# Where the maxima of the first softmax are taken: VectorE alone, or ScalarE, GpSimd and VectorE in turn

## The chip, the cores and the metric

The kernel runs on one core of a Trainium2 chip. The core has five engines that run beside each other: TensorE (PE in the profile) for matrix products, VectorE (DVE), ScalarE (ACT), GpSimd (POOL), and SyncE (SP), which here only issues DMAs. Each works through its own queue in order. PE writes to PSUM; GpSimd reads and writes SBUF only. The metric is the device time of one execution in microseconds; lower is better.

## The reference

Two parts. First, for each of 4 batches of 12,416 tokens with 128 channels, an attention by way of 32 inducing points:

```python
def mab(q, kv):
    s = scale * (q @ kv.transpose(0, 2, 1))
    s = s - s.max(-1, keepdims=True)
    a = np.exp(s)
    a /= a.sum(-1, keepdims=True) + 1e-09
    return a @ kv
h = mab(I, x)          # 32 points read all tokens: the first softmax
y = mab(x, h)          # all tokens read the 32 results: the second softmax
```

Second, on all 49,664 rows of y, a gated layer of width 1536:

```python
gate = 1.0 / (1.0 + np.exp(-(y @ w_gate)))
out = (gate * (y @ w_val)) @ w_out
```

## The kernel before

Tokens come in chunks of 128, 97 to a batch: six groups of 16 chunks and one chunk left over. The first softmax of a batch ("stage 1") runs over whole groups: the scores of 16 chunks stand in one PSUM bank as 128 rows (four times 32 points) by 512 columns. `s1_max` (line 264) has VectorE take the negated maximum of each row, `s1_exp` has ScalarE take the exponential with that maximum as bias, a DMA on SP's queue transposes the result (`s1_turn_dma`, line 304), PE sums it against the tokens (`s1_sum_pe`, line 315), and ScalarE copies the sum to `hst` (line 330). Each group keeps its own maximum; `plan_combine` (line 416) later joins the seven with weights, for which VectorE takes `ml` and GpSimd does the small steps up to `hx` and `e32l`. PE (line 455) and VectorE (`li`, line 375) finish it.

The second softmax ("stage 2", `plan_stage2`, line 617) takes 16 chunks too. PE scores a group in two halves (line 483); in the slot called `take` ScalarE copies the scores to `sc` (line 520) and GpSimd subtracts the greatest of each 32 by a tree of subtract, clamp and add (`s2_lower_pool`, lines 530 to 535); in the slot `weigh` ScalarE takes the exponential (line 544); one slot on, GpSimd sums (line 552); three slots on, it inverts and spreads the result to four copies `a2n` (lines 576 to 598); five to eight slots on, SP issues the transposing DMA to `a2r` (line 609).

The gated layer is the main loop. It has 97 blocks of four chunks, each block 12 columns of 128 hidden units, cut into steps of two columns and one column in turn. A step t is: PE fills the value bank `v` of step t and the gate bank `g` of step t+2 (line 944), VectorE forms u = (t16 + 1) * v (line 981), ScalarE takes the tanh of gate t+2 into `t16` (line 962), and PE multiplies earlier products u by `w_out` (line 1062). At the end of a block ScalarE copies the sum to `o` (line 1081) and SP sends it out (line 1083). Two steps are one slot, four slots a block, 96 slots a batch.

The order of all queues is written out by hand. `at(slot, make, late)` puts work into a slot: the early kind is issued after the slot's first step, the late kind after its second. Within a slot the order is that in which the work was planned, and an engine's queue keeps it. Stage 1 of batch b+1 is planned into the loop of batch b, as are the loads of `xn` on GpSimd's queue (line 96), the transposes of `xn` to `xT` on SP's queue (line 105), stage 2 of groups 0 and 1 of batch b+1, and the joining. Stage 1 of the first batch is a prologue with an order of its own, and the loop's last batch has no stage 1; so the loop has 18 full groups of stage 1. In the last batch nine columns go `aside`: ScalarE and GpSimd form them in place of VectorE (lines 1015 to 1031).

Slots below are counted from the start of a batch's loop. What the steps of the prediction need of the old plan, for the first two batches: joining starts in slot 52 and `li` stands in slot 63; the loads of slot 60 are two; group 0 of the next batch is lowered in slot 70 and weighed in slot 78.

Of the kernel before, what the change touches and what calls it, by code (L numbers as in the profile page):

```python
# [9 lines left out]
F32 = mybir.dt.float32  # L10
F16 = mybir.dt.float16
BF16 = mybir.dt.bfloat16
AF = mybir.ActivationFunctionType
ALU = mybir.AluOpType
AX = mybir.AxisListType

AFTER = mybir.DependencyInfo(mybir.DependencyClass.Sync, mybir.DependencyReason.DATA)
P = 128
GC = 16
BC = 4  # L20
ASIDE = {3: ((2, 9, 3, 8), (11, 17, 7, 1), (23, 26, 7, 0), (50, 53, 15, 3), (58, 62, 19, 11), (64, 69, 19, 10), (73, 76, 20, 5), (78, 81, 23, 11), (83, 88, 23, 10))}
LATE = (4, 19, 32, 46, 43)
NEG = 1.0e30
PROLOGUE = """
    xt 0 0, xt 0 8, cp 0 8 act, cp 0 0, w 2 1, xt 1 0, cp 1 0, sc 0, mx 0, ex 0, sc 6, xt 1 8,
# [12 lines left out]
def kernel(  # L38
# [9 lines left out]
    nc = tc.nc  # L48
# [18 lines left out]
    bp = ctx.enter_context(tc.tile_pool(name="bp", bufs=2))  # L67
    s1p = ctx.enter_context(tc.tile_pool(name="s1p", bufs=4))
    s2p = ctx.enter_context(tc.tile_pool(name="s2p", bufs=2))
    up = ctx.enter_context(tc.tile_pool(name="up", bufs=6))  # L70
    tp = ctx.enter_context(tc.tile_pool(name="tp", bufs=4))
    op = ctx.enter_context(tc.tile_pool(name="op", bufs=4))

# [158 lines left out]
    def at(slot, make, late=False, side=False):  # L232
        plan.setdefault((slot, "side" if side else late), []).append(make)
# [98 lines left out]
    def plan_stage1(b, s, score, total):  # L332
        st = {}
        full = groups[s][1] == GC

        def begin():
# [11 lines left out]
        at(score, begin)  # L348
        at(score + 1, weigh, late=full)
        at(score + 2, turn)  # L350
# [266 lines left out]
    def plan_stage2(b, c, score, take, weigh, far=None, soon=False):  # L617
        st = {}
        n = GC + (NLO if far is not None else 0)

        def bank():
            st["s2"] = ps.tile([P, GC, m], F32, tag="m", name="s2_ps")

        def room():
            st["sc"] = s2p.tile([P, GC + NLO, m], F32, tag="sc", name="sc", bufs=1)

        def one():
            room()
            bank()
            s2_score(b, 0, 0, NLO, st["s2"], True)  # L630

        def half(j0, whole):
            if j0 == 0:
                bank()
            s2_score(b, c, j0, j0 + GC // 2, st["s2"], whole)
            if soon and j0:
                st["hl"] = s2_max(GC, st["s2"])

        def lower():
            if far is None:  # L640
                room()
            s2_take(st["sc"], 0, GC, st["s2"])
            s2_lower_pool(n, st["sc"])

        def exp():
            st["e"] = s2_exp(GC, st["s2"], *st["hl"]) if soon else s2_exp_low(n, st["sc"])

        def total():
            st["sme"] = s2_sum_pool(n, st["e"])

        def spread():
            rs = (s2_inverse if soon else s2_inverse_pool)(n, st["sme"])
# [437 lines left out]
    for b in range(B):  # L1090
        o = base[b]
        more = b + 1 < B

        if b == 0:
            plan_stage2(0, groups[1][0], o, None, o + 3, soon=True)
            plan_stage2(0, groups[2][0], o + 5, o + 7, o + 18)
        for s in range(3 if b == 0 else 2, NG - 1):
            k = o + (16 * s - 28 if more else LATE[s - 2])
            plan_stage2(b, groups[s][0], k, k + 2, k + (14 if more else 10))
        k = o + (56 if more else LATE[-2])  # L1100
        plan_stage2(b, groups[NG - 1][0], k, k + 2, k + 10, far=o + (52 if more else LATE[-1]))
        if not more:
            continue
        early = (
            [(9, (18, 19, 19)), (13, (27, 27, 27))]
            if b == 0
            else [(8, (15, 16, 17)), (12, (18, 19, 19))]
        )
        later = (
            [(24, (35, 35, 35)), (28, (43, 43, 43)), (40, (48, 49, 49)), (44, (50, 51, 51))]  # L1110
            if b == 0
            else [(24, (31, 31, 31)), (28, (35, 35, 35)), (40, (47, 48, 49)), (44, (50, 51, 51))]
        )
        alone = 47 if b == 0 else 43
        for s, (score, total) in enumerate(early + later + [(32, (alone, alone, alone))]):
            plan_stage1(b + 1, s, o + score, [o + e for e in total])
        plan_combine(b + 1, o + 52, o + 55, [(o + 72, o + 74), (o + 80, o + 82)])
        plan_stage2(b + 1, groups[0][0], o + 67, o + 70, o + 78)
        plan_stage2(b + 1, groups[1][0], o + 84, o + 86, o + 94)
        for g in range(NS):  # L1120
            when = 3 * g if b else (3, 7, 16, 21, 31, 37, 12)[g]
            at(o + when, lambda b=b, g=g: x_transpose_dma(b + 1, g))
            if b == 0 and 0 < g < NG:
                at(o + (None, 4, 5, 17, 24, 31)[g], lambda g=g: x_load(1, g))
        if b + 2 < B:
            for g in range(NG):
                when = ((24, 33, 42, 60, 60, 82) if b else (33, 37, 60, 60, 78, 82))[g]
                at(o + when, lambda b=b, g=g: x_load(b + 2, g))
# [62 lines left out]
```

## Time and profile before

| | us |
|---|---|
| median of 3 runs | 719.72 |
| lowest, highest | 719.56, 719.85 |
| span of the profiled execution | 718.4 |
| busy PE, VectorE, ScalarE, GpSimd | 650.5, 702.4, 675.1, 445.8 |

The page gives no time for the profiled execution beside its span, from the first to the last instruction; 1.3 us lie between it and the median of the runs. In rows of the order of time, the first number is the start and the second the length, in us from the start of the span; rows of one operation that follow each other are merged (x4 is four of them), and a bracket gives the engine's idle time before the row and what ended it. In rows by group, the two numbers behind the count are the busy time in us and the mean length in ns.

### The profile page before, as it was taken

The numbers are of one execution on the slowest core, as the hardware profiler recorded it, in microseconds if no ns is written. First come the engines' busy times: TensorE is split into PE (matmuls) and PEld (weight loads), VectorE is DVE, ScalarE is ACT, GpSimd is POOL, SyncE is SP. The second block draws the span as 40 slices with busy tenths as digits, with TensorE's granted clock in tenths as the row PEclk, the third lists the DMA queues.
The fourth block names the chain that finished last, engine by engine and source line by source line (L and its number), as shares of the span: only waits on it lengthen the run. The fifth ranks groups of instructions, "written<-read, shape, count | busy, mean of one in ns | idle before, by whom it ended". The sixth has DMA issues, their size and how long they took to land.

```text
span 718.4 us, 21566 instructions
## 1 busy us (share of the span) xinstructions
PE 650.5 (91%) x8446; PEld 394.2 (55%) x8446; DVE 702.4 (98%) x872; ACT 675.1 (94%) x1019; POOL 445.8 (62%) x718
## 2 busy tenths in 40 slices
PE   8889889999998998999989988999899999999897
PEld 4455555555555555555555555555555555555555
DVE  5899999999999999999999999999999999999997
ACT  4699999999999999999999999999999999999996
POOL 4574763888653747588666266387766787676220
PEclk9999999999999999999999999999999999999999
DMA  9796696244568344335268431220222122223011
GB/s 209 115 182 130 125 165 105 75 90 106 89 133 162 80 103 92 59 79 119 66 117 161 102 75 51 70 74 31 77 60 73 46 62 67 39 75 71 35 46 46
DMA packets 118182, 65.77 MB, mean 92 GB/s; under 512 B 101408, under 2 KB 102208, under 8 KB 118080
## 3 DMA queue, kind: packets, MB, share of 16 engines
q1 hardware_dynamic: 112176, 50.90, 31.6%
q0 software_dynamic: 5584, 13.34, 10.9%
q8 instruction: 66, 1.08, 0.6%
q14 instruction: 36, 0.29, 0.1%
q10 hardware_dynamic: 320, 0.15, 0.1%
HBM read 27.80 MB, written 25.43 MB: 74 GB/s over the span
## 4 chain that ended last, share of the span: by engine, by line
PE 51%; ACT 24%; DVE 16%; issue 5%; DMA 2%; DVEq 1%; POOL 1%; ACTq 0%
PE acc_ps L1062 24%; ACT t L962 22%; PE v_ps L944 21%; DVE u L981 14%; PE g_ps L944 2%; DMA xn<-in_x_dram 2%; PE s_ps L483 2%; PE hp_ps L315 1%; ACT o L1081 1%; DVE nm L267 1%; DVEq L981 1%; ACT a1T L280 0%; PE s_ps L255 0%; POOL xn L96 0%; ACTq L962 0%
## 5 line engine op out<-in xcount | busy, mean ns | idle before, releaser
L981 DVE SCALAR_TENSOR_TENSOR u<-t,v_ps 128x1024 f16<-128x1024 f16 (+1 forms) x771 | 670.9, 945 | 1.7 <-PE g_ps L944 0.8
L962 ACT ACTIVATE t<-g_ps 128x1024 f16<-128x1024 f32 (+1 forms) x770 | 589.5, 822 | 22.2 <-ACT t L962 10.3
L944 PE MATMUL v_ps<-a2r,hwt 32*128 32x512 f16 (+1 forms) x1179 | 290.8, 371 | 56.9 <-DVE u L981 53.2
L1062 PE MATMUL acc_ps<-wo,u 128*128 128x128 f16 x4620 | 324.5, 220 | 0.9
L1062 PEld LDWEIGHTS <-u 128*128 128x128 f16 x4620 | 259.9, 98 | 89.5 <-issue 88.1
L944 PE MATMUL g_ps<-a2r,hwt 32*128 32x512 f16 (+1 forms) x1179 | 294.0, 376 | 0.0
L944 PEld LDWEIGHTS <-hwt 32*128 32x128 f16 x2382 | 93.5, 91 | 188.6 <-issue 142.2
L552 POOL TENSOR_TENSOR sum<-e 128x256 f32<-128x256 f16 (+1 forms) x23 | 15.5, 672 | 133.8 <-ACT e L544 130.0
L598 POOL TENSOR_TENSOR a2n<-e,rs 128x2048 f16<-128x2048 f16 (+3 forms) x25 | 86.8, 3474 | 4.8 <-DVE rs L570 3.1
L576 POOL TENSOR_TENSOR near<-sme,minus 128x16 f32<-128x16 f32 (+1 forms) x22 | 65.3, 2966 | 1.8
L1081 ACT ACTIVATE o<-acc_ps 128x512 f32<-128x512 f32 x96 | 58.4, 609 | 0.0
L531 POOL TENSOR_SCALAR rise<-rise 128x256 f32<-128x256 f32 (+6 forms) x110 | 51.2, 466 | 9.7
L532 POOL TENSOR_TENSOR top<-top,rise 128x128 f32<-128x128 f32 (+3 forms) x88 | 28.4, 323 | 7.3
L552 POOL TENSOR_TENSOR sum<-sum 128x128 f32<-128x128 f32 (+3 forms) x92 | 28.4, 309 | 7.2
L530 POOL TENSOR_TENSOR rise<-top 128x128 f32<-128x128 f32 (+3 forms) x88 | 27.3, 310 | 6.9
L530 POOL TENSOR_TENSOR rise<-sc 128x256 f32<-128x256 f32 (+1 forms) x22 | 16.3, 739 | 20.9 <-ACT sc L520 20.6
L1031 POOL TENSOR_TENSOR xn_spare<-xn_spare 128x512 f16<-128x512 f32 x9 | 11.4, 1270 | 22.2 <-ACT xn_spare L1029 22.0
L535 POOL TENSOR_TENSOR sc<-sc,top 128x512 f32<-128x512 f32 (+1 forms) x22 | 23.9, 1086 | 1.7
L1026 POOL TENSOR_SCALAR xn_spare<-xn_spare 128x512 f32<-128x512 f16 x9 | 13.4, 1493 | 11.2 <-ACT xn_spare L1025 11.2
L483 PEld LDWEIGHTS <-xT 128*128 128x128 f16 x388 | 13.1, 96 | 11.7 <-issue 11.3
L280 ACT ACTIVATE a1T<-s_ps,nm 128x512 f16<-128x512 f32 (+1 forms) x26 | 16.4, 630 | 3.1 <-DVE nm L267 3.0
L483 PE MATMUL s_ps<-hT,xT 128*128 128x32 f16 x388 | 18.1, 178 | 0.1
(150 smaller groups left out, 291.4 us busy)
## 6 DMA issues: line engine op xcount, KB each, us to landing
out_dram<-o SPq DMA_DIRECT2D x96, 256.0 KB, 2.2
xn<-in_x_dram POOLq DMA_DIRECT2D x18, 512.0 KB, 7.7
xn<-in_x_dram POOLq DMA_DIRECT2D x3, 544.0 KB, 6.9
xn<-in_x_dram POOLq DMA_DIRECT2D x3, 256.0 KB, 12.8
xn<-in_x_dram SPq DMA_DIRECT2D x1, 576.0 KB, 4.8
xn<-in_x_dram SPq DMA_DIRECT2D x1, 512.0 KB, 3.9
a2r<-a2n SPq DMA_TRANSPOSE x29, 4.5
wg<-in_moe_w_gate_dram POOLq DMA_DIRECT2D x1, 384.0 KB, 12.7
```

The source lines that it names most:

```text
L483: nc.tensor.matmul(s2[:, j, :], xT[b][:, c + j, :], hT16[b][:], start=(j == 0), stop=whole and j == j1 - 1, skip_group_check=True,)
L530: nc.gpsimd.tensor_tensor(out=r, in0=far, in1=near, op=ALU.subtract)
L531: nc.gpsimd.tensor_scalar_max(out=r, in0=r, scalar1=0.0)
L532: nc.gpsimd.tensor_tensor(out=top[:, 0:n, 0:w], in0=near, in1=r, op=ALU.add)
L552: nc.gpsimd.tensor_tensor(out=d[:, 0:n, :], in0=src[:, :, 0:w], in1=src[:, :, w : 2 * w], op=ALU.add)
L576: nc.gpsimd.tensor_tensor(out=near[:, 0:n], in0=sme[:, 0:n], in1=minus1[:, 0:n], op=ALU.pow)
L598: eng.tensor_tensor(out=a2n[:, 0:n, :, :], in0=e.unsqueeze(2).to_broadcast((P, n, 4, m)), in1=rs.unsqueeze(2).unsqueeze(3).to_broadcast((P ...
L944: st[what + "end"] = nc.tensor.matmul(pt[:, k, col : col + nb * P], hw[b][r : r + 32, j // 2, :], a2r[r : r + 32, o : o + nb, :].rearrange ...
L962: st["tanh"] = nc.scalar.activation(out=st["t"][:], in_=st["g"][:], func=AF.Tanh, scale=0.5)
L981: u = nc.vector.scalar_tensor_tensor(out=st["u"][:, :, c:e], in0=st["t"][:, :, c:e], scalar=1.0, in1=st["v"][:, :, c:e], op0=ALU.add, op1= ...
L1062: nc.tensor.matmul(acc[0][(i // 2) % len(acc[0])][:, i, :], u[:, ts(i, P)], wo16[:, j, :], start=(i in fresh), stop=not any(e[2] == ib and ...
L1081: nc.scalar.mul(out=o32[:], in_=acc[0][0][:], mul=0.5)
```

## The change

For 13 of the 18 groups the scores stay in PSUM only for one copy: ScalarE writes them, negated, to SBUF (`neg`, 128x512 in fp32) in the slot of the scores. GpSimd folds the 512 columns to 256, 128 and 64 by taking the smaller of two each time (`lower_tree`: subtract, clamp at zero, subtract; nine instructions). VectorE then takes the minimum of the 64 columns left (`finish`), which is the negated maximum that it took before from 512 columns. The exponential reads `neg` with scale -1 (`weigh_low`). Such a group has a list of six slots: score, minimum, exponential, and three for the sum. The other five groups keep the old way and four slots.

All slots move into one table, `TIMES`. Stage 2, the joining and the loads keep their slots. The first group of the third and of the fourth batch is scored 35 slots before the loop of the batch ahead of it begins, and so late in the batch before that; its `xT` transpose goes 38 slots before, behind whatever stands in that slot. The pools `up`, `tp` and `op` lose two, one and one buffers a tag; `neg` and `low1` have four.

```diff
+TIMES = (
+    {
...
+        "sum": ((10, 17, 26, 31, 31, 31), (14, 20, 30, 35, 35, 35), (27, 36, 42, 48, 48, 48), (28, 43, 43, 43), (40, 49, 49, 49), (44, 50, 50, 50), (32, 47, 47, 47)),
...
+        "turn": (3, 7, 16, 21, 31, 37, 12),
+    },
+    {
...
+        "sum": ((-35, -28, -6, -1, -1, -1), (2, 8, 11, 16, 16, 16), (10, 17, 26, 30, 30, 30), (14, 20, 30, 35, 35, 35), (27, 36, 42, 47, 47, 47), (44, 50, 50, 50), (32, 43, 43, 43)),
+        "join": (52, 55, (72, 74), (80, 82)),
+        "next": ((67, 70, 78), (84, 86, 94)),
+        "turn": (-38, -4, 3, 6, 14, 18, 16),
+    },
...
-    up = ctx.enter_context(tc.tile_pool(name="up", bufs=6))
-    tp = ctx.enter_context(tc.tile_pool(name="tp", bufs=4))
-    op = ctx.enter_context(tc.tile_pool(name="op", bufs=4))
+    up = ctx.enter_context(tc.tile_pool(name="up", bufs=4))
+    tp = ctx.enter_context(tc.tile_pool(name="tp", bufs=3))
+    sp = ctx.enter_context(tc.tile_pool(name="sp", bufs=1))
+    op = ctx.enter_context(tc.tile_pool(name="op", bufs=3))
...
+    def lower_tree(low, neg):
+        w, src = 2 * P, neg
+        rise1 = s2p.tile([P, (GC + NLO) * (m // 2)], F32, tag="sum16", name="rise1")
+        top1 = s2p.tile([P, (GC + NLO) * (m // 2)], F32, tag="sum16", name="top1")
+        while w >= LOW:
+            near, far = src[:, 0:w], src[:, w : 2 * w]
+            r = rise1[:, 0:w]
+            nc.gpsimd.tensor_tensor(out=r, in0=near, in1=far, op=ALU.subtract)
+            nc.gpsimd.tensor_scalar_max(out=r, in0=r, scalar1=0.0)
+            dst = low if w == LOW else top1
+            nc.gpsimd.tensor_tensor(out=dst[:, 0:w], in0=near, in1=r, op=ALU.subtract)
+            src = dst
+            w //= 2
...
+        def fill():
+            st["s1"] = s1_score_pe(b, s, "m")
+
+        def leave():
+            st["neg"] = sp.tile([P, 4 * P], F32, tag="neg", name="neg", bufs=4)
+            st["low"] = sp.tile([P, LOW], F32, tag="low1", name="low1", bufs=4)
+            nc.scalar.mul(out=st["neg"][:], in_=st["s1"][:], mul=-1.0)
+            lower_tree(st["low"], st["neg"])
+
+        def finish():
+            nm, _, col = s1_col(b, s)
+            nc.vector.tensor_reduce(
+                out=nm[:, col], in_=st["low"][:], axis=AX.X, op=ALU.min
+            )
+
+        def weigh_low():
+            nm, _, col = s1_col(b, s)
+            st["a1T"] = s1p.tile([P, 512], F16, tag="a1T", name="a1T")
+            nc.scalar.activation(
+                out=st["a1T"][:], in_=st["neg"][:], func=AF.Exp, bias=nm[:, col], scale=-1.0
+            )
+
+        if pooled:
+            done, weight, *total = total
+            at(score, fill)
+            at(score, leave, late=True)
+            at(done, finish)
+            at(weight, weigh_low, late=True)
+            at(weight + 1, turn)
+        else:
...
-            when = 3 * g if b else (3, 7, 16, 21, 31, 37, 12)[g]
-            at(o + when, lambda b=b, g=g: x_transpose_dma(b + 1, g))
+            at(o + times["turn"][g], lambda b=b, g=g: x_transpose_dma(b + 1, g))
```

More of the change, by code (lines that the diff above doesn't have):

```diff
@@ L21 @@
 ASIDE = {3: ((2, 9, 3, 8), (11, 17, 7, 1), (23, 26, 7, 0), (50, 53, 15, 3), (58, 62, 19, 11), (64, 69, 19, 10), (73, 76, 20, 5), (78, 81, 23, 11), (83, 88, 23, 10))}
-LATE = (4, 19, 32, 46, 43)
+TIMES = (
+    {
+        "late": {2: (5, 7, 18, None), 3: (20, 22, 34, None), 4: (36, 38, 50, None), 5: (56, 58, 66, 52)},
+        "sum": ((10, 17, 26, 31, 31, 31), (14, 20, 30, 35, 35, 35), (27, 36, 42, 48, 48, 48), (28, 43, 43, 43), (40, 49, 49, 49), (44, 50, 50, 50), (32, 47, 47, 47)),
[4 more added lines that the diff above has]
+    {
+        "late": {2: (4, 6, 18, None), 3: (20, 22, 34, None), 4: (36, 38, 50, None), 5: (56, 58, 66, 52)},
+        "sum": ((-35, -28, -6, -1, -1, -1), (2, 8, 11, 16, 16, 16), (10, 17, 26, 30, 30, 30), (14, 20, 30, 35, 35, 35), (27, 36, 42, 47, 47, 47), (44, 50, 50, 50), (32, 43, 43, 43)),
+        "join": (52, 55, (72, 74), (80, 82)),
+        "next": ((67, 70, 78), (84, 86, 94)),
+        "turn": (-38, -4, 3, 6, 14, 18, 16),
+    },
+    {
+        "late": {2: (4, 6, 14, None), 3: (19, 21, 29, None), 4: (32, 34, 42, None), 5: (46, 48, 56, 43)},
+    },
+)
+LOW = 64
 NEG = 1.0e30
@@ L330, in s1_sum_keep, with plan_stage1 @@
         nc.scalar.copy(out=hsts[b % 2][0:R, at_col[s], 0:width], in_=hp[0:R, 0:width])
[L332 removed]
+    def lower_tree(low, neg):
[11 more added lines that the diff above has]
+            w //= 2
+    def plan_stage1(b, s, score, *total):
         st = {}
         full = groups[s][1] == GC
+        pooled = len(total) > 3
         def begin():
@@ L346, in turn @@
                 st["a1"] = s1_turn_copy(s, s1_turn_pe(b, s, st["a1T"]))
-        at(score, begin)
-        at(score + 1, weigh, late=full)
-        at(score + 2, turn)
+        def fill():
[15 more added lines that the diff above has]
+                out=st["a1T"][:], in_=st["neg"][:], func=AF.Exp, bias=nm[:, col], scale=-1.0
+            )
+        if pooled:
[6 more added lines that the diff above has]
+        else:
+            at(score, begin)
+            at(score + 1, weigh, late=full)
+            at(score + 2, turn)
         first, second, keep = total
@@ L1092 @@
         more = b + 1 < B
+        times = TIMES[min(b, 1) if more else 2]
         if b == 0:
             plan_stage2(0, groups[1][0], o, None, o + 3, soon=True)
[L1096 to L1101, printed above, removed]
+        for s, (*slots, far) in times["late"].items():
+            plan_stage2(b, groups[s][0], *(o + k for k in slots), far=None if far is None else o + far)
         if not more:
             continue
[L1104 to L1119, printed above, removed]
+        for s, slots in enumerate(times["sum"]):
+            plan_stage1(b + 1, s, *(o + k for k in slots))
+        plan_combine(b + 1, *(o + k for k in times["join"][:2]), [(o + f, o + k) for f, k in times["join"][2:]])
+        for s in range(2):
+            plan_stage2(b + 1, groups[s][0], *(o + k for k in times["next"][s]))
         for g in range(NS):
-            when = 3 * g if b else (3, 7, 16, 21, 31, 37, 12)[g]
-            at(o + when, lambda b=b, g=g: x_transpose_dma(b + 1, g))
+            at(o + times["turn"][g], lambda b=b, g=g: x_transpose_dma(b + 1, g))
             if b == 0 and 0 < g < NG:
```

## The prediction

> **What bounds the kernel now.** I read the page first: busy time by engine, then the chain that ended last.
>
> ```profile
> span 718.4 us, 21566 instructions
> ...
> PE 650.5 (91%) x8446; PEld 394.2 (55%) x8446; DVE 702.4 (98%) x872; ACT 675.1 (94%) x1019; POOL 445.8 (62%) x718
> ...
> PE 51%; ACT 24%; DVE 16%; issue 5%; DMA 2%; DVEq 1%; POOL 1%; ACTq 0%
> ```
>
> The chain names PE most, because every product starts from a matmul that was itself released by the product before. The busy times say who sets the pace. By stretches of the steady loop:
>
> ```profile
> 140.00:310.00 170.00, 154.45 (x2057) 93.96 (x2056) 170.00 (x204) 164.08 (x246) 110.73 (x184) 1.00 0.49 102
> ```
>
> Columns: stretch, length, then busy time and instructions of PE, weight load, DVE, ACT, POOL, then granted clock and DMA. VectorE has no idle time, ScalarE seems nearly full, GpSimd is two thirds busy, the clock is full. So VectorE work taken out of these stretches shortens them, as long as nobody arrives later than before. What one maximum costs shows in the order of time:
>
> ```profile
> 360.34 0.60 ACT L1081 ACTIVATE o<-acc_ps 128x512 f32<-128x512 f32 x1
> 367.25 0.60 ACT L1081 ACTIVATE o<-acc_ps 128x512 f32<-128x512 f32 x1
> ...
> 388.00 0.60 ACT L1081 ACTIVATE o<-acc_ps 128x512 f32<-128x512 f32 x1
> 395.52 0.60 ACT L1081 ACTIVATE o<-acc_ps 128x512 f32<-128x512 f32 x1
> ```
> ```profile
> 387.68 0.68 DVE L267 TENSOR_REDUCE nm<-s_ps 128x1 f32<-128x512 f32 x1
> 388.28 6.99 DVE L981 SCALAR_TENSOR_TENSOR u<-t,v_ps 128x512 f16<-128x512 f16 x8
> ```
>
> One output copy ends each block of four slots. A block without a maximum takes 6.91 us (1.73 a slot), one with a maximum 7.52: 0.61 more, and the next product starts 0.60 after the maximum did, though its record is 0.68 long (the ends of VectorE records overlap by 0.08).
>
> **The change, part by part.**
>
> *VectorE.* 13 maxima go, 13 minima over 64 columns in SBUF come. The two nearest reductions:
>
> ```profile
> L424 DVE TENSOR_REDUCE ml<-nm 128x1 f32<-128x7 f32 x3 | 0.5, 153 | 0.0
> L267 DVE TENSOR_REDUCE nm<-s_ps 32x1 f32<-32x128 f32 x4 | 1.1, 271 | 0.0
> ```
>
> 7 columns take 153 ns and 128 take 271, so 64 take some 0.21 us by a straight line, 0.13 without the overlap. Saved: 0.60 - 0.13 = 0.47 each, 13 x 0.47 = 6.1 us (5.3 to 6.8 with 0.19 or 0.08 for the new one).
>
> *ScalarE.* 13 copies come. How much room there is shows where ScalarE is fullest, in the last batch:
>
> ```profile
> 558.46 0.60 ACT L1081 ACTIVATE o<-acc_ps 128x512 f32<-128x512 f32 x1
> 558.94 1.53 ACT L962 ACTIVATE t<-g_ps 128x1024 f16<-128x1024 f32 x2
> 560.32 0.63 ACT L1029 COPY xn_spare<-side_v_ps 128x512 f32<-128x512 f32 x1
> ...
> 627.25 0.60 ACT L1081 ACTIVATE o<-acc_ps 128x512 f32<-128x512 f32 x1
> ...
> 634.45 0.64 ACT L1081 ACTIVATE o<-acc_ps 128x512 f32<-128x512 f32 x1
> ```
>
> A 512-column operation holds ScalarE 0.48 (558.46 to 558.94), a slot's two gates 1.38 (558.94 to 560.32). Against 1.73 a slot it has 0.35 to spare, 1.4 a block: room for the output copy and nearly two more. The 94% of the page overstates it, for the same overlap. But two extras in one block, as between 627.25 and 634.45, made 7.20 of 6.91: crowding costs up to 0.29. The 13 copies (6.2 us of ScalarE) fall mostly in blocks with none or one extra; copy, exponential and `hst` copies meet in a block about twice a batch. I take 0.6 us, ends 0 and 13 x 0.29 = 3.8. The exponential now reads SBUF instead of PSUM. The rows have 635 ns for one from SBUF and 683 from PSUM (another bias), so I count no change, ends -0.6 and +0.6 us in all, inside the ends above.
>
> ```profile
> L280 ACT ACTIVATE a1T<-s_ps,nm 128x512 f16<-128x512 f32 x22 | 15.0, 683 | 3.1 <-DVE nm L267 3.0
> L544 ACT ACTIVATE e<-sc 128x512 f16<-128x512 f32 x18 | 11.4, 635 | 0.0
> ```
>
> [...]
>
> *GpSimd.* Each tree is nine instructions on 256, 128 and 64 columns, the same three widths with which the second softmax's tree begins. One whole such stretch, and its place in GpSimd's queue around slots 60 to 79 of the first batch:
>
> ```profile
> 150.47 1.21 POOL L96 DMA_DIRECT2D xn<-in_x_dram  x2
> 152.41 0.69 POOL L552 TENSOR_TENSOR sum<-e 128x272 f32<-128x272 f16 x1 [0.74 <-ACT e L544]
> ...
> 163.03 0.73 POOL L530 TENSOR_TENSOR rise<-sc 128x256 f32<-128x256 f32 x1
> ...
> 168.54 0.24 POOL L530 TENSOR_TENSOR rise<-top 128x32 f32<-128x32 f32 x1
> ...
> 170.57 1.07 POOL L535 TENSOR_TENSOR sc<-sc,top 128x512 f32<-128x512 f32 x1
> ...
> 173.19 0.66 POOL L552 TENSOR_TENSOR sum<-e 128x256 f32<-128x256 f16 x1 [0.94 <-ACT e L544]
> ```
>
> 163.03 to 168.54: 5.5 us a tree (5.2 if flat operands run like the 128x258 addition, 644 ns instead of 733), 72 us in all. It is free wherever GpSimd waits, and mid-batch it does. At the end of a batch it does not: between 150.47 and 173.19 its only pauses are the two in brackets. The tree of the next batch's group 0 (score at -35, that is slot 61) is queued right behind the two loads of slot 60. It starts at 151.68 at best and ends at 157.2, so the sum behind it starts 4.8 late (5.5 less the 0.74 pause), and so does the lowering of `sc`, which then ends at 171.64 + 4.8 = 176.4 instead of 171.64. ScalarE's exponential of slot 78 needs it:
>
> ```profile
> 172.47 0.63 ACT L544 ACTIVATE e<-sc 128x512 f16<-128x512 f32 x1
> 172.99 1.51 ACT L962 ACTIVATE t<-g_ps 128x1024 f16<-128x1024 f32 x2
> ```
> ```profile
> 174.47 1.81 DVE L981 SCALAR_TENSOR_TENSOR u<-t,v_ps 128x1024 f16<-128x1024 f16 x2
> ```
>
> It would start at 176.4, 3.9 late. Behind it in ScalarE's queue is the gate that ends about 174.02 and is used by VectorE at 174.47: 0.45 of cover. So VectorE loses 3.4 us. The same place of the second batch:
>
> ```profile
> 322.87 0.69 POOL L552 TENSOR_TENSOR sum<-e 128x272 f32<-128x272 f16 x1 [0.72 <-ACT e L544]
> ...
> 341.03 1.07 POOL L535 TENSOR_TENSOR sc<-sc,top 128x512 f32<-128x512 f32 x1
> ```
> ```profile
> 343.05 0.63 ACT L544 ACTIVATE e<-sc 128x512 f16<-128x512 f32 x1
> ```
>
> Lowering ends at 342.10 + 4.8 = 346.9, 3.85 late, 3.4 after cover. Together 6.8 us (6.2 with the shorter tree, 0 if something not seen hides it, 7.8 without cover). Nothing of the gain falls between slots 50 and 80, so the delay is not paid by it.
>
> Two earlier waits lie inside these 3.4 and are not added. First, the minimum of slot 68 stands in VectorE's order ahead of all products behind it:
>
> ```profile
> 144.56 0.41 PE L455 MATMUL lh_ps<-e32l,ones 128*128 128x32 f32 x2
> 145.83 0.35 DVE L375 RECIPROCAL li<-lh_ps 128x32 f32<-128x32 f32 x1
> ```
> ```profile
> 137.22 1.83 SPq L609 DMA_TRANSPOSE a2r<-a2n  x1
> ```
> ```profile
> DMA to landing us min/median/max: 4.1/4.4/5.1
> ```
>
> `li` is slot 63, so slot 68 is at 145.83 + 0.37 + 5 x 1.73 = 154.9, while the tree ends at 157.2: a wait of 2.4. Second, the transposing DMA of slot 58 stands on SP's queue behind the `a2r` of 137.22 (it waits for GpSimd), starts at 139.05 and lands 4.4 later (transposes of `xT`, second batch), at 143.5. PE wants it at slot 61, 144.56 - 2 x 1.73 = 141.1. PE, then VectorE, would lose one to two of the 2.4.
>
> The other moved or delayed things. The trees of slots 10 and 14 push the load of slot 17 in the first batch from 55.48 to 66.5:
>
> ```profile
> 55.48 0.61 POOL L96 DMA_DIRECT2D xn<-in_x_dram  x1
> ```
> ```profile
> xn<-in_x_dram POOLq DMA_DIRECT2D x18, 512.0 KB, 7.7
> ```
> ```profile
> 81.83 0.40 PE L255 MATMUL s_ps<-xT,indT 128*32 128x512 f16 x4
> ```
>
> It lands about 74.8, its transpose holds SP till then and lands at 79.2; the scores of slot 28 want it at 81.83 - 1.4 (three savings) = 80.4. One late load costs up to 3; I take 0.6 for this and for `a1` transposes that now have three or four slots instead of five. The other trees meet their minima. The tightest is that of slot 2 with its minimum in slot 8, where a maximum stood before:
>
> ```profile
> 207.41 3.61 POOL L598 TENSOR_TENSOR a2n<-e,rs 128x2048 f16<-128x2048 f16 x1
> ```
> ```profile
> 217.10 0.68 DVE L267 TENSOR_REDUCE nm<-s_ps 128x1 f32<-128x512 f32 x1
> ```
>
> It starts at 211.02, behind the spreading, and ends at 216.5, half a microsecond ahead. Moving the remaining `xT` transposes and the shallower `up`, `tp`, `op` pools I cost at nothing: by the pacing in `project` a product is read within five steps, and four buffers of each size cover eight.
>
> Sum: -6.1 + 6.8 + 0.6 + 0.6 = +1.9 us. The page gives the span alone, 718.4, so 720.3; the runs' median, 719.72, is 1.3 longer, and I set the forecast against it: 721.6.
>
> **The rivals.**
>
> *The last tree is hidden: faster.* If the lowering of slot 70 still ends within the cover, 6.8 falls away: 719.7 - 6.1 + 1.2 = 714.8. It decides at a tree of 0.74 + 0.83 + 0.45 = 2.0 us (pauses before the sum and between lowering and exponential, then cover). Rows of these widths say 5.5, so against; what speaks for it is that the rows are of strided operands and the new ones are flat. Chance 0.22. [...]
>
> *Half hidden: about no change.* A shorter tree, more cover, or only one of the two places: 6.8 becomes 3.4 to 5, and the time 718 to 720. Chance 0.15.
>
> *ScalarE or the loads become the bound.* Crowding of 0.29 at most copies and a late load: 719.7 - 6.1 + 6.8 + 2.5 + 1.8 = 724.7. For it: the two-extra block; against: 1.4 of room a block. Chance 0.18.
>
> **How the numbers follow.** My forecast, 721.6, has 0.45, with a range of its own of 720 to 723.5; about 0.13 of that lies within 0.2% (1.4 us), about what a measurement of this kernel tells from no change. With the half-hidden case split evenly: faster 0.22 + 0.07 = 0.29, same 0.13 + 0.08 = 0.21, slower 0.32 + 0.18 = 0.50. The range 715.8 to 726 leaves out most of the hidden case and the worst of the loads.
>
> **What would show it.** Right: 13 reductions of 128x64 near 0.2 us; blocks of the removed maxima at 7.05 instead of 7.52; idle VectorE of 2 to 4 us at slots 61 to 80 of the first two batches, with `low1`, GpSimd or `xT` named as releaser, and the exponential of slot 78 late. Wrong: no VectorE idle there (the hidden case), idle spread evenly with ScalarE as releaser (the ScalarE case), or a stall of PE on `xT` or `a1` in the first batch.

## The result, and the profile after

| | before | after |
|---|---|---|
| median of the runs, us | 719.66 | 731.75 |
| lowest, highest | 719.56, 719.85 | 727.11, 732.61 |
| span of the profiled execution | 718.4 | 725.3 |

The change makes the kernel slower: ratio 1.0155, 95% interval 1.013 to 1.018. The forecast was 721.6 with a range of 715.8 to 726, so the sign was right and the size was not. A second set of executions of the same kernel gave 730.32 us (728.45 to 732.63; ratio 1.0139, interval 1.0104 to 1.0174). The executions of the changed kernel scatter over 5 us, where the five of the old one agree within 0.3 (of 57 later ones of the old kernel 55 lie between 719.1 and 721.1, and two, at a mean clock of 0.989, at 723.3 and 723.4); the scatter turns out to be part of the answer. The profile shown for the changed kernel is that of its fastest execution, 727.11 us.

The page of the changed kernel, busy times and shares of the chain by engine:

```profile
PE 658.9 (91%) x8446; PEld 399.0 (55%) x8446; DVE 699.3 (96%) x872; ACT 679.3 (94%) x1032; POOL 507.5 (70%) x835
...
PE 47%; ACT 24%; DVE 17%; DMA 5%; issue 4%; POOL 1%; DVEq 1%; ACTq 0%; POOLq 0%
```

VectorE is 3.1 us less busy than before, so work did leave it, but it now stands idle for 26.0 us of the span instead of 16.0. DMA has 5% of the chain instead of 2%. The groups by line show the new operations, and what VectorE's products wait for (the first line stands alone, it is the kernel before):

```profile
L981 DVE SCALAR_TENSOR_TENSOR u<-t,v_ps 128x1024 f16<-128x1024 f16 (+1 forms) x771 | 670.9, 945 | 1.7 <-PE g_ps L944 0.8
```
```profile
L394 DVE TENSOR_REDUCE nm<-low 128x1 f32<-128x64 f32 x13 | 2.7, 210 | 0.0
L401 ACT ACTIVATE a1T<-neg,nm 128x512 f16<-128x512 f32 x13 | 9.5, 731 | 0.0
L1046 DVE SCALAR_TENSOR_TENSOR u<-t,v_ps 128x1024 f16<-128x1024 f16 (+1 forms) x771 | 673.8, 948 | 12.5 <-PE g_ps L1009 9.4
L275 PE MATMUL s_ps<-xT,indT 128*32 128x512 f16 (+1 forms) x100 | 10.7, 382 | 6.3 <-DMA xT<-xn 5.7 <-ACT neg L389 0.6
```

The wait on a gate bank from PE (`g_ps`) was 0.8 us before and is 9.4 now, and PE's waits on a late `xT` are 5.7, which were none. Slot 61 of the first batch, where the next batch's group 0 is scored, in the order of time: SP's queue, PE and VectorE.

```profile
137.12 1.91 SPq L674 DMA_TRANSPOSE a2r<-a2n  x1
139.13 2.59 SPq L125 DMA_TRANSPOSE xT<-xn  x1
```
```profile
143.88 0.40 PE L275 MATMUL s_ps<-xT,indT 128*32 128x512 f16 x4 [2.86 <-DMA xT<-xn]
...
144.63 1.46 PE L1127 MATMUL acc_ps<-wo,u 128*128 128x128 f16 x12
```
```profile
144.80 0.69 DVE L1046 SCALAR_TENSOR_TENSOR u<-t,v_ps 128x512 f16<-128x512 f16 x1 [2.50 <-PE g_ps L1009]
146.67 1.22 DVE L1046 SCALAR_TENSOR_TENSOR u<-t,v_ps 128x1024 f16<-128x1024 f16 x1 [1.18 <-PE g_ps L1009]
```

The transpose of `xT` starts at 139.13, as soon as SP is past `a2r`, and lands 4.7 us later; PE wanted it at 141.0. The gate and value matmuls of the following steps stand behind these scores in PE's queue, so VectorE stands still for 2.50. Then comes a second gap of 1.18, for which no wait on data is to be seen: the twelve `acc_ps` matmuls take 1.46 us where they take 0.84 elsewhere. Stretches around it give the reason (columns as in the prediction's stretch; the granted clock is the third number from the end):

```profile
140.00:142.00 2.00, 1.02 (x16) 0.71 (x14) 2.00 (x3) 2.00 (x4) 1.74 (x4) 1.00 1.13 209
142.00:144.00 2.00, 0.12 (x4) 0.10 (x3) 0.30 (x1) 0.33 (x1) 1.82 (x3) 1.00 1.09 270
144.38:147.79 3.41, 3.41 (x28) 2.13 (x27) 1.80 (x2) 2.11 (x4) 2.82 (x8) 0.50 0.02 5
148.00:150.00 2.00, 2.00 (x26) 1.40 (x23) 1.93 (x4) 1.62 (x3) 1.67 (x5) 1.00 0.00 0
```

PE did nothing from 141.0 to 143.9, and from 144.38 to 147.79 the clock granted to it was half. PE was busy all that time, while VectorE had work for 1.80 of the 3.41 us. The second batch has the same at 318 us: PE waits 2.85 us for `xT`, and from 318.46 the clock is half for 3.41 us.

To compare whole batches I use the stretch from one `ml` of VectorE to the next: it holds all loop work of one batch once. Before it is 170.45 and 170.59 us in the two full batches, after 174.07 and 173.71.

```profile
126.74:297.19 170.45, 154.78 (x2061) 94.07 (x2059) 170.45 (x204) 164.51 (x247) 111.10 (x185) 1.00 0.50 103
```
```profile
126.59:300.66 174.07, 158.29 (x2061) 96.15 (x2058) 169.08 (x205) 166.55 (x253) 135.02 (x230) 0.99 0.49 100
```

Before, VectorE has no idle time in it (170.45 of 170.45). After, it has 5.0.

### The profile page after: what moved, and what is told of

Same layout as the page of the kernel before. It is cut to its first block, busy times and chain, and to the rows that moved or that the text cites. A ratio compares the mean times of both kernels' runs of the same rounds, so it can differ in the third digit from the quotient of the medians.

```text
span 725.3 us, 21726 instructions
## 1 busy us (share of the span) xinstructions
PE 658.9 (91%) x8446; PEld 399.0 (55%) x8446; DVE 699.3 (96%) x872; ACT 679.3 (94%) x1032; POOL 507.5 (70%) x835
## 4 chain that ended last, share of the span: by engine, by line
PE 47%; ACT 24%; DVE 17%; DMA 5%; issue 4%; POOL 1%; DVEq 1%; ACTq 0%; POOLq 0%
PE acc_ps L1127 23%; ACT t L1027 21%; PE v_ps L1009 19%; DVE u L1046 15%; PE g_ps L1009 3%; DMA a<-a1T 2%; DMA xn<-in_x_dram 2%; ACT o L1146 1%; DMA xT<-xn 1%; PE hp_ps L335 1%; PE s_ps L548 1%; DVEq L1046 1%; DMA a2r<-a2n 1%; PE s_ps L275 1%; ACT sc L585 0%
## 5 line engine op out<-in xcount | busy, mean ns | idle before, releaser
L1027 ACT ACTIVATE t<-g_ps 128x1024 f16<-128x1024 f32 (+1 forms) x770 | 589.6, 823 | 25.3 <-ACT t L1027 10.2
L1009 PEld LDWEIGHTS <-hwt 32*128 32x128 f16 x2382 | 96.0, 91 | 181.9 <-issue 133.5
L360 POOL TENSOR_SCALAR rise<-rise 128x256 f32<-128x256 f32 (+2 forms) x39 | 22.6, 579 | 3.4
```

Source lines behind the costliest of these rows:

```text
L1009: st[what + "end"] = nc.tensor.matmul(pt[:, k, col : col + nb * P], hw[b][r : r + 32, j // 2, :], a2r[r : r + 32, o : o + nb, :].rearrange ...
L1027: st["tanh"] = nc.scalar.activation(out=st["t"][:], in_=st["g"][:], func=AF.Tanh, scale=0.5)
```

## The experiments

**The changed kernel again, unaltered.** It shows what differs between two executions of one program.

> The changed kernel once more, unaltered. Its five executions lay at 727.1 and at 731.0 to 732.6 us, with mean granted clocks of 0.995 and 0.983 to 0.986. Theory (PE stalls at slot 61 on the late xT transpose, and the granted clock falls behind the stall): a profile of an execution near 731 shows more time at about half clock than the 7 us of the profile at 727, and all of it starts at such stalls. Rival (the time differs for a reason of its own, in GpSimd or in the DMAs): a profile near 731 has the same stretches at a low clock as the one at 727 and longer waits elsewhere.

Measured: median 730.32 us; the execution with the profile took 732.63, span 730.9. VectorE, and then two stretches, at the same place:

```profile
145.39 0.69 DVE L1046 SCALAR_TENSOR_TENSOR u<-t,v_ps 128x512 f16<-128x512 f16 x1 [2.90 <-PE g_ps L1009]
147.25 1.82 DVE L1046 SCALAR_TENSOR_TENSOR u<-t,v_ps 128x1024 f16<-128x1024 f16 x2 [1.18 <-PE g_ps L1009]
149.61 1.22 DVE L1046 SCALAR_TENSOR_TENSOR u<-t,v_ps 128x1024 f16<-128x1024 f16 x1 [0.54 <-PE g_ps L1009]
...
153.09 1.22 DVE L1046 SCALAR_TENSOR_TENSOR u<-t,v_ps 128x1024 f16<-128x1024 f16 x1 [1.19 <-PE g_ps L1009]
```
```profile
143.27:156.93 13.66, 12.81 (x94) 7.79 (x93) 8.08 (x11) 7.72 (x11) 11.81 (x26) 0.50 0.45 92
156.93:160.00 3.07, 2.77 (x40) 1.72 (x39) 2.83 (x4) 2.52 (x5) 0.48 (x2) 1.00 0.42 124
```

The stall is nearly the same, but the clock stays at half for 13.7 us instead of 3.4 (in the second batch for 10.2 instead of 3.4), and VectorE has four gaps of 0.45 or more behind it instead of one. The two batch stretches are 177.12 and 176.02, 2.3 to 3.1 above those of the faster execution. The theory held: the scatter goes with the time for which the clock stays low. The mean clocks of all nine executions agree with it: 0.995 at 727.1 us, 0.991 and 0.989 at 728.5 and 729.2, 0.983 to 0.986 from 731.0 up.

**The first group's scores four slots later.** This gives `xT` time to land. The group's tree keeps its place in GpSimd's queue, behind the loads of slot 60.

```diff
-        "sum": ((-35, -28, -6, -1, -1, -1), ...
+        "sum": ((-31, -24, -6, -1, -1, -1), ...
```

> Only the first group's slots move: scored at -31 instead of -35, minimum at -24 instead of -28 (slots 65 and 72). PE then finds its xT landed; the tree's place in GpSimd's queue, behind the two loads of slot 60 and ahead of the sum of slot 67, is unchanged. Theory A (PE's stall and the low clock behind it cost about 4.0 us at each of two places, GpSimd's backlog would cost 3.4 there by itself and is hidden beneath): 725 to 726.5 us, clock 1.00, no spread between executions, VectorE idle around slot 78 with ScalarE's exponential of slot 78 waiting for GpSimd. Theory B (the stall alone, GpSimd's backlog costs nothing): 718 to 720. Theory C (backlog alone): no change, 727 to 732.

Measured: 729.84 us (728.56 to 730.38), ratio 1.0128 [1.0102, 1.0155]. The wait on `xT` at slot 61 is gone, and in its place stands the one that the prediction had put first: the exponential of slot 78 waits for GpSimd's lowering. ScalarE's group, VectorE, and stretches:

```profile
L609 ACT ACTIVATE e<-sc 128x512 f16<-128x512 f32 (+1 forms) x22 | 14.2, 646 | 7.1 <-POOL sc L600 7.1
```
```profile
177.56 1.22 DVE L1046 SCALAR_TENSOR_TENSOR u<-t,v_ps 128x1024 f16<-128x1024 f16 x1 [3.23 <-issue]
179.22 0.69 DVE L1046 SCALAR_TENSOR_TENSOR u<-t,v_ps 128x512 f16<-128x512 f16 x1 [0.43 <-PE g_ps L1009]
181.09 1.82 DVE L1046 SCALAR_TENSOR_TENSOR u<-t,v_ps 128x1024 f16<-128x1024 f16 x2 [1.18 <-PE g_ps L1009]
```
```profile
174.00:176.00 2.00, 0.17 (x2) 0.00 (x0) 0.33 (x1) 0.07 (x1) 1.75 (x5) 1.00 0.00 0
...
178.00:180.00 2.00, 2.00 (x18) 1.17 (x17) 1.47 (x2) 1.55 (x2) 1.67 (x5) 0.50 0.99 197
```

So the queue delay of 3.4 us a place that the prediction worked out is real: 7.1 us of ScalarE over two places, 3.23 of VectorE at the first. The expectation of 725 to 726.5 fell all the same: PE stands still here too, for 3.35 us, and behind that the clock is halved for 6.8 us. By its time alone this run would also fit theory C, that GpSimd's backlog does it all; the next run decides that.

**The old way for the first group, at the same slot.** The tree goes, the early `xT` stays.

```diff
-        "sum": ((-35, -28, -6, -1, -1, -1), ...
+        "sum": ((-35, -1, -1, -1), ...
```

> The first group of the third and fourth batch goes back to the old way (VectorE takes the maximum of 512 columns in the slot of the scores, no copy, no tree), but still in slot -35. PE's stall on the late xT stays, GpSimd's extra tree at the end of a batch goes. Theory A: the stall alone, 727 to 732 plus 2 x 0.47, so 728 to 733, with the clock below 1 as before. Theory C (GpSimd's backlog alone): 720 to 721, clock 1.00.

Measured: 729.86 us (727.09 to 731.61), ratio 1.0123 [1.0082, 1.0164]. VectorE waits 2.23 for the late scores and then 1.18, 0.54 and 1.18 at a clock of 0.50. The stall on `xT` therefore needs no tree: theory A held, and the backlog of GpSimd alone does not explain the kernel.

**Both causes away.** The first group is scored after the lowering of slot 70 has been issued.

```diff
-        "sum": ((-35, -28, -6, -1, -1, -1), ...
+        "sum": ((-17, -10, -6, -1, -1, -1), ...
```

> The first group pooled as in the change, but scored at -17 with the minimum at -10 (slots 79 and 86), where GpSimd has pauses of 3.0 and 5.3 us; both suspected causes go. Theory A: 727.1 - 2 x 4.05 = 719.0 us, clock 1.00, no spread; what is still missing from the 713.6 that the saved VectorE time alone would give (5 us) is lost inside the batches. Theory B the same. Theory C the same; if it stays above 723, the cause is somewhere else than at the end of the batches.

Measured: 719.66 us (718.7 to 720.59), ratio 0.9994 [0.9983, 1.0006], clock 1.00. One batch:

```profile
126.86:297.44 170.58, 156.84 (x2061) 95.45 (x2058) 168.95 (x204) 166.32 (x253) 134.59 (x230) 1.00 0.49 103
```

All of the slowdown stands at the two ends of batches. (The execution with the profile took 720.59, the longest of the ten, so its stretches are on the long side.) But the 6.1 us saved on VectorE are not there either: 719.7 - 6.1 would be 713.6. By batch, five maxima at 0.47 should have made 170.45 into 168.1, and it is 170.58 and 170.34. The next runs look for these 6 us.

**The shallower pools alone, in the kernel before.**

```diff
-    up = ctx.enter_context(tc.tile_pool(name="up", bufs=6))
-    tp = ctx.enter_context(tc.tile_pool(name="tp", bufs=4))
-    op = ctx.enter_context(tc.tile_pool(name="op", bufs=4))
+    up = ctx.enter_context(tc.tile_pool(name="up", bufs=4))
+    tp = ctx.enter_context(tc.tile_pool(name="tp", bufs=3))
+    op = ctx.enter_context(tc.tile_pool(name="op", bufs=3))
```

> The kernel before, with nothing but the shallower pools of the change (up 4, tp 3, op 3 buffers a tag). The prediction's step: they cost nothing, so 719.7 within 0.4 us. Rival: part of the 6 us that are still lost with both end-of-batch causes away comes from here, 721 to 726.

Measured: 719.79 us, ratio 1.0002 [0.9993, 1.0011]. The pools cost nothing.

**Both causes away, and the 13 copies left out.** Tree and exponential read one constant tile.

```diff
-            st["neg"] = sp.tile([P, 4 * P], F32, tag="neg", name="neg", bufs=4)
+            st["neg"] = negc
...
-            nc.scalar.mul(out=st["neg"][:], in_=st["s1"][:], mul=-1.0)
```

> The kernel with the first group moved to slots -17 and -10 (719.7 us), with ScalarE's 13 copies left out: tree and exponential read one tile of SBUF that is written once, so the maxima and weights of these groups are not those of the scores. Trees, minima, exponentials and all DMAs stay. Theory (ScalarE's added copies crowd it and give back the 6 us that VectorE's saved time should bring): 714 to 716 us. Rival (late a1 transposes, PE's own work in slots that had a pause of VectorE before, or GpSimd): 718.5 to 720.

Measured: 716.87 us (716.71 to 717.14), ratio 0.996 [0.9948, 0.9973].

```profile
126.87:295.83 168.96, 156.18 (x2061) 95.01 (x2057) 168.63 (x204) 164.04 (x248) 134.81 (x230) 1.00 0.47 103
```

The copies, with what waits for them, cost 719.66 - 716.87 = 2.8 us; in a full batch 170.58 - 168.96 = 1.6 for five, by a long execution of the one and a usual one of the other. The time lies between the two forecasts: about half of the missing 6 us is the copies.

**Both causes away, and the exponentials two or three slots earlier.** A late `a` had been seen at 94 us.

```diff
-        "sum": (..., (14, 20, 30, 35, 35, 35), ...          # first table
+        "sum": (..., (14, 20, 27, 35, 35, 35), ...
-        "sum": (..., (14, 20, 30, 35, 35, 35), ..., (44, 50, 50, 50), ...   # second table
+        "sum": (..., (14, 20, 28, 35, 35, 35), ..., (44, 51, 51, 51), ...
```

> The same kernel with more room for three transposes of a1: the exponential of group 1 three slots earlier (27 for 30) in the first table and that of group 3 two slots earlier (28 for 30) in the second, and the sum of group 5 one slot later (51 for 50) in the second. The profile of the change shows PE waiting for a late a1 three times, with VectorE idle 0.35 us behind it each time. Theory (these are a part of the 6 us): 718.3 to 719.2 us. Rival (they are not, or the exponentials crowd ScalarE more at the new place): 719.4 to 720.5.

Measured: 720.8 us (ten executions from 720.27 to 722.04, one at 1690.02 of which no trace was kept), ratio 1.0016 [1.0006, 1.0025]; against the 719.66 of the version that it alters, 1.1 slower (1.6 by the two ratios). The forecast that more room for `a` gains time fell, but the run does not price late `a` by itself. PE's wait on the DMA of `a`, 0.3 us in the version that it alters, is gone. In its place ScalarE is late with other things, as the rival had it: an exponential now stands directly ahead of the copy `neg` at 81 us, for which PE waits 1.20, and directly ahead of the output copy at 255 us, and VectorE waits 0.81 behind that, in two batches.

**The copies alone, in the kernel before** (with the shallower pools). Thirteen copies of scores go to a tile that nobody reads; maxima and exponentials are the old ones.

```diff
+        def leave():
+            neg = sp.tile([P, 4 * P], F32, tag="neg", name="neg", bufs=4)
+            nc.scalar.mul(out=neg[:], in_=st["s1"][:], mul=-1.0)
...
+        if full and s < (3 if b == 1 else 5):
+            at(score, leave, late=True)
```

> The kernel before with the shallower pools and with the 13 copies added to its own plan (ScalarE writes the negated scores to SBUF in the slot of the scores; nothing reads them, VectorE takes its maxima as before). ScalarE's room is 1.4 us a block and a maximum gives 0.6 more. Theory (a copy costs only where VectorE no longer stops for a maximum): 719.7 to 721. Rival (a copy costs its 0.48 us wherever it stands): 13 x 0.48 = 6.2, so 724 to 726.

Measured: 724.95 us (724.61 to 725.26), ratio 1.0072 [1.0059, 1.0085]: 5.2 us for 13 copies, 0.40 each. The rival held: a copy costs nearly the 0.48 for which it holds ScalarE, though VectorE still stops for the maxima. Here the copy stands next to the group's exponential, which is one slot on.

**The changed kernel with PE kept busy in the stall.** Before the late scores PE does eleven matmuls whose result is overwritten.

```diff
+            if s == 0 and b > 1:
+                for _ in range(11):
+                    nc.tensor.matmul(s1[:], ident[:], xT[b - 1][:, 0:4, :], start=True, stop=True)
             st["s1"] = s1_score_pe(b, s, "m", s1)
```

> The changed kernel, with one thing added: at the two places where PE waits for the late xT (scores of the next batch's first group, slot 61) it first does eleven matmuls of 128x512 whose result is overwritten, about 2.4 us at full clock by the acc_ps rows (0.07 us per 128 columns in a row of twelve), so that it stands still 0.5 us instead of 2.9. The wait itself stays. Theory A, that the time lost behind the stall is a cost of its own and comes from PE standing still: the granted clock stays at 1.00 behind the stall, VectorE loses 2.5 to 3 us at each place and nothing of 0.4 or more behind it, the stretch from ml to the maximum of slot 8 is about 93 us (90.4 before), and the time is 724 to 726.5 with a spread under 1.5 between executions. Rival B, that the clock falls whatever PE does at that place: clock at or below 0.7 behind the stall, 728 to 732. Rival C, that the stall on xT is all and the clock only goes with it: VectorE's waits of 1.18 and 0.5 behind the stall stay with the clock at 1.00, and 727 or more.

Measured: 726.41 us, five executions within 726.11 to 726.54 and one at 729.53, whose mean clock is 0.99; ratio 1.0093 [1.0074, 1.0113]; clock of the profiled one 1.00. PE and VectorE:

```profile
141.12 2.55 PE L387 MATMUL s_ps<-xT,ident 128*128 128x512 f16 x11
144.12 0.40 PE L275 MATMUL s_ps<-xT,indT 128*32 128x512 f16 x4 [0.45 <-DMA xT<-xn]
```
```profile
144.94 0.69 DVE L1050 SCALAR_TENSOR_TENSOR u<-t,v_ps 128x512 f16<-128x512 f16 x1 [2.48 <-PE g_ps L1013]
145.98 2.95 DVE L1050 SCALAR_TENSOR_TENSOR u<-t,v_ps 128x1024 f16<-128x1024 f16 x3 [0.35 <-PE g_ps L1013]
...
178.16 1.82 DVE L1050 SCALAR_TENSOR_TENSOR u<-t,v_ps 128x1024 f16<-128x1024 f16 x2 [0.51 <-issue]
180.24 41.13 DVE L1050 SCALAR_TENSOR_TENSOR u<-t,v_ps 128x1024 f16<-128x1024 f16 x47 [0.27 <-PE g_ps L1013]
```

The stall is as long as ever, 2.48 against 2.50, but the gaps of 1.18 and 0.54 behind it are gone, and with them nearly all the scatter. PE has more work in this kernel than in the changed one and the kernel is 3.9 to 5.3 us faster by the medians of the two sets. Theory A held in the clock and in the time; that the clock falls whatever PE does, fell. It missed in one point: it expected no wait of 0.4 or more behind the stall, and 93 us from `ml` to the minimum of slot 8. A wait of 0.51 at slot 78 came, and the stretch is 94.5. At full clock the two lateness causes share the end of the batch: 2.48 + 0.35 = 2.83 at slot 61 and 0.51 + 0.27 = 0.78 at slot 78.

**Copies and exponentials of the 13 groups left out** (both causes away). The transposing DMA of `a` reads a tile of ones.

```diff
-            st["a1T"] = s1p.tile([P, 512], F16, tag="a1T", name="a1T")
-            nc.scalar.activation(
-                out=st["a1T"][:], in_=st["neg"][:], func=AF.Exp, bias=nm[:, col], scale=-1.0
-            )
+            st["a1T"] = a1c
```

> The kernel of e5 (both stalls away, and the 13 copies of negated scores left out) with the exponentials of the same 13 groups left out too: the transposing DMA of a1 reads a tile of ones. ScalarE then has 26 operations less than in e3 and 13 less than in the kernel before. Theory A, that the 3.3 us missing behind e5 are ScalarE's, its exponentials standing closer to its other work in the new slots: 712.5 to 714.8. Rival B, that PE's sums, late a1 or the loads are what is late: 716 to 717.

Measured: twelve executions from 716.05 to 730.8 us, median 724.8, outside both forecasts. As a time this settles nothing: in the profiled execution, 719.45 us, a transposing DMA of `a` lands late in the first batch, PE stands still for 2.08, and the clock falls to 0.50. PE there, and the stretch at half clock:

```profile
94.87 0.30 PE L339 MATMUL hp_ps<-xn,a 128*32 128x128 f16 x4 [2.08 <-DMA a<-a1c]
```
```profile
94.20:101.03 6.83, 6.16 (x84) 3.89 (x84) 2.77 (x5) 3.02 (x6) 6.09 (x10) 0.50 1.08 234
```

The later batches are at full clock, and there the comparison is clean:

```profile
129.57:298.11 168.54, 155.08 (x2061) 94.50 (x2058) 168.44 (x204) 161.87 (x243) 134.74 (x230) 1.00 0.48 104
```

168.54 and 168.55 against 168.96 and 168.95 with the exponentials: five of them cost 0.4 in their new slots. What is left above 168.1 is 0.4 a batch, though VectorE counts as busy for 168.44 of 168.54. VectorE at the end of this batch:

```profile
269.50 0.21 DVE L397 TENSOR_REDUCE nm<-low 128x1 f32<-128x64 f32 x1
269.63 13.90 DVE L1046 SCALAR_TENSOR_TENSOR u<-t,v_ps 128x512 f16<-128x512 f16 x16
283.46 0.68 DVE L291 TENSOR_REDUCE nm<-s_ps 128x1 f32<-128x512 f32 x1
284.06 14.13 DVE L1046 SCALAR_TENSOR_TENSOR u<-t,v_ps 128x512 f16<-128x512 f16 x16
298.11 0.15 DVE L489 TENSOR_REDUCE ml<-nm 128x1 f32<-128x7 f32 x1
```

A minimum holds VectorE for 0.13 (269.50 to 269.63) and a maximum for 0.60 (283.46 to 284.06), so a pair is worth the predicted 0.47. The rest is in the products. Sixteen of them take 13.83 from 269.63 and 14.05 from 284.06: they wait a little, and because records overlap by 0.08, waits of that size show no idle time. By the starts of the products in the batch, such delays behind a late gate bank of PE come to 0.58 us, against 0.15 in the same batch of the kernel before; the difference is the 0.4.

**A version with fewer pooled groups,** in slots that are meant to hold no other extra work of ScalarE.

```diff
-        "sum": ((-35, -28, -6, -1, -1, -1), (2, 8, 11, 16, 16, 16), (10, 17, 26, 30, 30, 30), (14, 20, 30, 35, 35, 35), (27, 36, 42, 47, 47, 47), (44, 50, 50, 50), (32, 43, 43, 43)),
+        "sum": ((-6, -1, 2, 8, 8, 8), (10, 17, 42, 47, 47, 47), (14, 20, 46, 51, 51, 51), (24, 31, 31, 31), (28, 35, 35, 35), (40, 49, 49, 49), (32, 43, 43, 43)),
```

> A version that is meant to keep what the change gains: e3's first batch, and in the third and fourth batch only three groups pooled instead of four, with no copy ahead of the batch, and ScalarE's copies and exponentials put into slots that hold no other extra work of ScalarE. 11 minima in place of 11 maxima save 11 x 0.47 = 5.2 of VectorE. Theory A, that what the copies and exponentials cost depends on what stands beside them in the slot: no stall at the ends of batches, losses inside batches 2 to 4 us instead of 6, 717 to 718.8. Rival B, that each moved group costs ScalarE about 0.45 us wherever it stands: 11 x 0.45 = 5, so 719.3 to 720.

The expectation miscounts: the table pools three groups of the third and fourth batch instead of five, so nine in all, worth 9 x 0.47 = 4.2, and the first group's copy does stand six slots ahead of the batch. Measured: 718.23 us (717.7 to 719.06), ratio 0.9975 [0.9966, 0.9983] to the kernel before. It is the one complete version that beats it. 719.9 - 4.2 = 715.7, so 2.5 us are lost, 0.28 a group instead of 6.1 / 13 = 0.47. The time lies where theory A had it. A full batch, where three pairs at 0.47 off 170.45 would be 169.0:

```profile
126.19:295.93 169.74, 155.52 (x2061) 94.43 (x2058) 169.65 (x204) 165.52 (x251) 125.37 (x212) 1.00 0.51 103
```

## Why the prediction was wrong, step by step

The account, in us. The two halves of the miss are of about one size:

| | predicted | measured | from |
|---|---|---|---|
| maxima off VectorE | -6.1 | -6.1 (0.47 x 13) | starts of rows, maximum and minimum |
| copies | 0.6 | 2.8 | copies left out |
| exponentials | 0 | about 1.1 (0.42 x 13 / 5) | batch with and without them |
| rest inside batches: late `a` and loads, small waits | 0.6 | about 2.2 | what is left to 719.7 |
| two ends of batches, full clock | 6.8 | 6.75 | 726.41 - 719.66 |
| half clock behind the stalls | - | 0.7 to 6.2, median 5.3 | 727.11 to 732.61, median 731.75, less 726.41 |

The 2.2 are what is left over; no run of their own settles them. Much of it seems to lie in the first batch: with the copies left out, the first `ml` stands at 126.87 us, where it stood at 126.74 before, though three pairs should have brought it 1.4 forward (executions differ here by some 0.6: 126.17 in the run of the pools alone). PE waits in that run 0.3 for `a` and 0.8 for `xT`.

*The step that failed first: "PE, then VectorE, would lose one to two of the 2.4", and what was not in it.* The prediction saw the stall: the transpose behind `a2r`, start 139.05, landing 143.5, wanted at 141.1. The trace has 139.13, 143.8 and 141.0. It took the stall for delay alone, and delay at one place that covers delay at the next. At full clock that was right: with PE kept busy the two ends cost 6.75 together where 6.8 were forecast. That the sums agree so well is partly luck: slot 61 was to cost one to two of the 3.4 a place and slot 78 the rest, and VectorE loses 2.83 at slot 61, nearly all of PE's wait, and 0.78 at slot 78. What it did not consider is what comes behind PE's standstill: after 2.86 us without work the granted clock falls from 1.00 to 0.50, and PE, which is 91% busy at full clock, cannot keep up with VectorE at half (twelve `acc_ps` matmuls take 1.46 us instead of 0.84). VectorE then waits for `g_ps` until the clock is back. The stretch shown before, with clock 1.00 everywhere, held no gap from which that could have been read; the prediction priced no such case, not even as a rival, and its range ended where this begins. One of its own signs of being wrong, a stall of PE on `xT` in the first batch, is what the trace shows at 141 us.

*The term that was mis-sized: ScalarE, 0.6.* "Room for the output copy and nearly two more" was worked out for a block of four slots. It does not hold when two extras come within a slot or two of each other. ScalarE of the changed kernel in two blocks of the second batch's loop:

```profile
214.63 0.60 ACT L1146 ACTIVATE o<-acc_ps 128x512 f32<-128x512 f32 x1
...
218.09 0.59 ACT L585 COPY sc<-s_ps 128x512 f32<-128x512 f32 x1
...
221.55 0.60 ACT L1146 ACTIVATE o<-acc_ps 128x512 f32<-128x512 f32 x1
...
225.13 0.60 ACT L389 ACTIVATE neg<-s_ps 128x512 f32<-128x512 f32 x1
...
226.99 0.75 ACT L401 ACTIVATE a1T<-neg,nm 128x512 f16<-128x512 f32 x1
227.60 1.54 ACT L1027 ACTIVATE t<-g_ps 128x1024 f16<-128x1024 f32 x2
228.99 0.65 ACT L1146 ACTIVATE o<-acc_ps 128x512 f32<-128x512 f32 x1
```

One extra: 214.63 to 221.55, 6.92. A copy and an exponential: 221.55 to 228.99, 7.44, about half a microsecond lost (a minimum on VectorE at 221.22 can be 0.13 of it). The upper end that I had written, 13 x 0.29 = 3.8, holds the 2.8 of the copies. What was wrong is how often they meet other work ("about twice a batch"), or what a meeting costs (0.4 here, not 0.29); the runs do not separate the two. The same copies cost 0.40 each beside the old exponentials and about 0.2 each in this table. Where the slots were chosen (the last version), copies and exponentials and all else together lose 0.28 a group.

*Steps that held.* The minimum over 64 columns takes 0.21 and the next product starts 0.13 after it, as the straight line said. The tree at slot 61 starts at 151.59 and the sum behind it at 157.11 (151.68 and 157.2 predicted):

```profile
151.59 0.75 POOL L359 TENSOR_TENSOR rise<-neg 128x256 f32<-128x256 f32 x1
...
157.11 0.70 POOL L617 TENSOR_TENSOR sum<-e 128x272 f32<-128x272 f16 x1
...
175.26 1.08 POOL L600 TENSOR_TENSOR sc<-sc,top 128x512 f32<-128x512 f32 x1
```

The lowering ends at 176.34 (176.4 predicted). That it delays ScalarE by only 0.22 there is no contradiction: everything else had already been moved back by the stall at slot 61, and with that stall taken away the wait appears, 7.1 us of ScalarE over two places. The minimum of slot 68 makes no one wait, for the same reason. The pools cost nothing.

*A term put at nothing: the exponential from SBUF.* "I count no change" was read from two rows with different biases. Its record is longer than that of one from PSUM, 731 ns against 683. How long it holds ScalarE shows where ScalarE has no pause behind it: 0.61 here (226.99 to 227.60), and 0.57 for one from PSUM in the run with the copies alone:

```profile
220.78 0.71 ACT L281 ACTIVATE a1T<-s_ps,nm 128x512 f16<-128x512 f32 x1
221.35 4.71 ACT L969 ACTIVATE t<-g_ps 128x1024 f16<-128x1024 f32 x6
```

So 13 of them cost ScalarE 13 x 0.04 = 0.5 us, which lies inside the end of +0.6 that the prediction gave this term.

*The rivals.* The nearest was "ScalarE or the loads become the bound", 724.7 at 0.18. Its ScalarE half was right in kind. The hidden tree and the half-hidden one did not occur: the tree takes 5.5, and where its delay is covered, in the changed kernel, it is the longer stall at slot 61 that covers it.

## What to carry to other kernels

Where VectorE sets the pace and PE is 91% busy, a stall on PE as long as those measured here (2.08 to 3.35 us) is not paid once: ask of every new wait whether PE runs dry behind it, and price PE's work at half clock behind it, here for 3.4 to 13.7 us. A transfer asked for early must be looked at in the queue in which it stands, since one place further back it comes too late for the scores that were moved ahead (here by 2.86 us). And room on an engine in order is to be counted by slot and not by block: 0.5 us of ScalarE work cost nothing alone in its block (6.92 against 6.91), and 0.4 of its 0.48 beside another.

## What the runs showed of the hardware that was not expected

In these traces the clock granted to TensorE fell to 0.50 at every pause of PE from 2.08 us (the run without exponentials) to 3.35 us (the scores four slots later). Pauses of 1.20 us (the exponentials two or three slots earlier) and 1.48 us (the start of the run without copies), and one cut to 0.45 by matmuls without use, left it at 1.00; nothing between 1.48 and 2.08 was measured. How long it stays low does not follow from the pause: pauses of 2.85 to 2.91 us were followed by 3.41 us at half clock in one execution and by 13.7 and 10.2 in another of the same program. All nine stretches at half clock behind these pauses, in five traces, last one, two, three or four times 3.41 us (3.41, 6.83, 10.24, 13.65).

What sets this step of 3.41 us, and with it the difference between two executions of one program, no run here shows. Why the clock takes up to four such steps to return is open too. Work for PE does not bring it back at once: in the run with the old way for the first group PE was busy for 10.00 of the 10.00 us from 320 to 330 us, all of them at a clock of 0.50.
